# Four row tiles: adding the bonus term on TensorE, copying out on ScalarE, loading g as one row, and a new order of the steps

## The chip, the cores and the metric

The kernel runs on one core of a Trainium2 chip. The core has five engines that run side by side and meet only through semaphores: TensorE (PE in the profile; it multiplies matrices and writes the results to PSUM), VectorE (DVE), ScalarE (ACT), GpSimd (POOL) and SyncE (SP, which here only issues DMAs). The metric is the device time of one execution in microseconds. The median of three runs of the kernel before is 148.79 us (148.41 to 152.24).

## The reference

Two layers, one after the other. The first is a linear attention with a decaying state, over 4 batches, 8 heads, 768 positions and a head size of 48:

```
for t in range(S):
    cur = einsum('bhd,bhe->bhde', u * k[t], v[t])
    y[t] = einsum('bhd,bhde->bhe', r[t], state + cur)
    state = w * state + einsum('bhd,bhe->bhde', k[t], v[t])
x = y, heads side by side: (4, 768, 384)
```

The second normalises each row of x and puts it through two matrices:

```
xn = (x - mean(x)) / sqrt(var(x) + 1e-6) * g_ln
out = x + relu(xn @ w_ch1) @ w_ch2        # 384 -> 1536 -> 384
```

All inputs and the output are fp32.

## The kernel before

**Tiling.** The 4 x 768 rows are cut into 24 chunks of 128 rows, 6 to a batch. Within a chunk the recurrence is solved by matrix products: k and r are scaled by powers of w (steps SK, SR), turned so that the head size lies on the partitions (TRk, TRr on TensorE with a copy out by TCk, TCr, or TDk, TDr by DMA), multiplied (AT) and masked (AM); S builds what the chunk adds to the state, ZU and ZD scale it, and Y multiplies masked products and state with v. What position t itself gives through u is a number cc per row and head (made by TensorE from q = k * r in S, copied out by CC2), times v: that product is Vb (step VB2). Step X adds Vb to y while copying y out of PSUM, with the sum of each row as by-product in sm; the result is x. Chunks are loaded in pairs. The first two pairs (chunks 0 to 3) have a layout of their own, in which a partition holds two neighbouring rows; their steps have a 2 at the end of the name (AT2, AM2, Y2, SR2, SK2; for the first pair SRH and SKH, by halves).

**The second layer.** SQ (ACT) takes the sum of squares of x minus the mean, RS the root, XN makes the centred x in bf16, LT and XT turn it (or LTD by DMA); chunks are grouped by one or two (GROUPS). UP multiplies with w_ch1, RL applies the relu out of PSUM into hT, DN multiplies hT with w_ch2, OT scales by RS and adds x, STO stores. UP,16*g+m is the m-th tile of 512 columns of group g; DN,4*i+d is the d-th third of the sum of chunk i. w_ch1 is loaded in three thirds by LW1 on SP's queue and scaled by -g in nine pieces by SW (piece 3*n+kc belongs to third n), on the engine that the plan names. w_ch2 is loaded in three thirds by IW2 on POOL's queue, with a conversion to bf16. g is loaded by LG (line 218) as 128x3, one element at a time, and negated by UGC (line 304).

**The order.** PLAN (lines 18 to 67) is a list of 755 steps, each with a name, an index and an engine (v DVE, s ACT, g POOL, - for TensorE or SP's queue). The kernel is emitted in just this order, so each engine's and each queue's own order is the order of its steps in the list; nothing is reordered later. DU,n is filler for TensorE: n/512 products of 128x512 zeros on line 279. Work ahead of the first UP is called the prologue below.

**Buffers.** The names y, o, hp and at are PSUM tiles: one buffer each for y and o, two each for hp and at. S and Y share y; UP, the products Y2 and the early rows WBM (line 288, an fp32 product that spreads ln w over 128 partitions) and COL (line 315, small fp32 products that turn rows into columns) share hp; AT, AT2 and all transpositions share at. A step that writes such a buffer waits for the readers of the tile before in it. The SBUF rings have the lengths in SLOTS.

**Lines.** Line 205 holds all products of two tensors (SK, SR, Q2, ZU), 200 and 202 all copies on ACT and on DVE or POOL, 342, 344 and 346 SW on ACT, DVE and POOL, 492 VB2, 590 X, 597 SQ, 646 UP, 674 DN. w_f and w_sb in the rows are the fp32 and bf16 weights.

Of the kernel before, what the change touches and what calls it, by code (L numbers as in the profile page):

```python
# [32 lines left out]
DN,2,- RS,2,g LT,5,- S,7,- OT,0,v RL,66,s UP,49,- XN,6,s XT,5,v UP,50,- RL,49,v TCr,4,s LR2,6,- DN,4,- ZU,7,v UP,80,-
ZD,7,v LK,10,- CV2,4,g RL,50,v Y,7,- RL,80,s DN,5,- X,7,v LV,13,- DN,6,- Q2,4,v XN,7,s UP,65,- SQ,4,s OT,1,v LV,11,-
AT,8,- SQ,6,s SR2,6,v AT,9,- DN,8,- RS,6,s LR2,5,- AM,8,v RS,4,s DN,9,- SQ,7,s LK,11,- S,8,- DN,10,- ZU,8,v LV,10,-
UP,82,- CC2,4,s OT,2,v VB2,4,g LK,12,- LT,6,- AM,9,v Y,8,- RL,82,s DN,12,- STO,0,- RL,65,s SK,10,g DN,13,- XT,6,v LK,13,-
X,8,v DN,14,- ZD,8,g LV,12,- S,9,- UP,96,- OT,3,v SK,11,g ZU,9,v UP,98,- RL,96,s SR2,5,v Y,9,- TDk,5,- SQ,8,s DN,16,-
CV2,5,v LT,7,- TRr,5,- SK,12,v DN,17,- X,9,v TCr,5,s RL,98,v LK,15,- UP,97,- XN,9,g LK,14,- XT,7,v ZD,9,g UP,81,- RL,97,s
LR2,7,- XN,8,s SK,13,g UP,112,- RL,81,s LTD,8,- DN,18,- RS,7,s Q2,5,v TRr,6,- OT,4,v UP,114,- SK,15,g TCr,6,s RL,112,v STO,1,-
S,10,- CV2,6,g DN,20,- CC2,5,s TDk,6,- RL,114,s SK,14,v AT,10,- RS,5,s AT,11,- ZU,10,v DN,21,- SR2,7,g AM,10,v UP,113,- STO,3,-  # L40
DN,22,- AM,11,v RL,113,s TDk,7,- Y,10,- VB2,5,g UP,129,- OT,5,v TRr,7,- RL,129,s LR,19,- UP,130,- ZD,10,g X,10,v UP,133,- LV,14,-
Q2,6,v RL,130,s DN,24,- TCr,7,v STO,2,- S,12,- DN,25,- CC2,6,s LV,15,- XN,10,s VB2,6,g ZU,12,v AT,12,- SQ,9,s AT,13,- STO,5,-
AM,12,v Y,11,- RL,133,s DN,26,- Q2,7,g LK,16,- X,11,v UP,128,- OT,6,v XN,11,s Y,12,- UP,131,- X,12,v LK,17,- DN,28,- AM,13,v
SR,19,g CV2,7,s S,13,- DN,29,- LTD,9,- ZU,13,v SQ,12,s DN,30,- ZD,13,g RL,128,s Y,13,- OT,7,v AT,15,- SQ,11,s LR2,8,- AT,14,-
X,13,v UP,132,- STO,4,- SK,17,g RL,131,v SQ,13,s LR,18,- S,14,- AM,15,v LV,17,- XN,13,s DN,32,- LV,16,- XN,12,s DN,33,- ZU,14,v
RL,132,s SK,16,v UP,144,- CC2,7,v AM,14,v LTD,10,- VB2,7,g UP,147,- RL,144,s DN,34,- SQ,10,s SR2,8,v TDk,8,- Y,14,- RS,8,s UP,145,-
RL,147,s OT,8,v TRr,8,- ZD,14,v UP,148,- TCr,8,s RL,145,v RL,148,v DN,36,- LK,18,- X,14,v DN,37,- CV2,8,v XN,14,s S,15,- UP,149,-
ZU,15,v LK,19,- UP,161,- ZD,15,g RL,149,v LV,18,- DN,38,- RL,161,s Q2,8,v STO,7,- Y,15,- LV,20,- UP,146,- SK,18,g X,15,v STO,6,-
AT,16,- RL,146,s AT,17,- XN,15,v LR,20,- UP,164,- RS,9,g OT,9,v LTD,11,- AM,17,v UP,160,- RL,164,s RS,10,g DN,40,- RL,160,v S,16,-
SK,19,v UP,163,- SR,18,v CC2,8,s TDk,9,- UP,165,- ZU,16,v RL,163,s AM,16,v DN,41,- ZD,16,g RL,165,s DN,42,- VB2,8,g LR,21,- UP,162,-  # L50
OT,10,v TDr,9,- Y,16,- RL,162,v DN,44,- X,16,v DN,45,- XN,16,g UP,176,- LV,19,- SR,20,g DN,46,- RL,176,s STO,8,- Y,17,- OT,11,v
UP,178,- LK,20,- X,17,v DN,48,- Q2,9,v LK,21,- UP,177,- XN,17,g SR,21,v DN,49,- LTD,12,- RL,177,s RL,178,v DN,50,- CV2,9,v AT,19,-
OT,12,v AT,18,- SK,20,g STO,9,- UP,180,- AM,18,v STO,11,- S,18,- SK,21,g RL,180,s UP,181,- CC2,9,v ZU,18,v DN,52,- VB2,9,g AM,19,v
# [4 lines left out]
UP,210,- AM,21,v RL,208,s DN,64,- SR,22,v S,20,- RL,210,v UP,212,- TDr,11,- CC2,10,v DN,65,- SK,22,v VB2,10,g ZU,20,v DN,66,- Y,20,-
TDk,11,- OT,16,v UP,209,- X,20,v DN,68,- RL,209,s ZD,20,v STO,14,- S,21,- XN,20,g RL,212,v CV2,11,s DN,69,- LTD,14,- ZU,21,v SQ,20,s
DN,70,- UP,213,- RS,13,s OT,17,v STO,16,- UP,211,- STO,15,- Y,21,- RL,211,s DN,72,- X,21,v DN,73,- Q2,11,v SQ,21,s AT,23,- ZD,21,v  # L60
RL,213,s AT,22,- XN,21,v S,22,- LTD,15,- UP,224,- ZU,22,v AM,22,v DN,74,- ZD,22,g RL,224,s UP,226,- CC2,11,s RS,14,s OT,18,v VB2,11,g
# [721 lines left out]
```

## Time and profile before

| | before |
|---|---|
| median of three runs | 148.79 us |
| profiled execution | 149.24 us |
| its span, first to last instruction | 147.5 us |
| TensorE busy | 141.5 us (96%) |
| VectorE busy | 112.3 us (76%) |
| ScalarE busy | 82.4 us (56%) |
| GpSimd busy | 72.0 us (49%) |
| share of the DMA engines, SP's queue | 78.3% |
| instructions | 4689 |

All rows are from one profiled execution; its span is 1.74 us shorter than its time. The ends of matmuls are modelled, so busy time of TensorE is not time at its peak: the distance from the start of one to the start of the next says more. A row of the order in time has start, length, engine, line, operation, result and operands, and how many were merged; in brackets stands the engine's idle time before it and what ended it.

### The profile page before, as it was taken

What the parts mean: (1) busy time and instruction counts of PE and PEld (TensorE: products, weight loads), DVE (VectorE), ACT (ScalarE), POOL (GpSimd) and SP (SyncE); (2) the same over time, 40 slices, a digit from 0 to 9 for tenths busy, and PEclk for the clock granted to TensorE, in tenths of its full rate; (3) what the DMA queues carried; (4) which work ended last, traced back from release to release, by engine and by line L of the source; (5) the groups of instructions that cost most, each with busy time, mean ns of one, the idle gap of its engine ahead of it and who ended that gap; (6) DMA issues with size and microseconds to landing.
All of it is one profiled execution on the core that took longest, in us unless ns stands there. A gap on an engine that the chain in (4) does not pass through costs nothing.

```text
span 147.5 us, 4689 instructions
## 1 busy us (share of the span) xinstructions
PE 141.5 (96%) x1943; PEld 111.1 (75%) x1943; DVE 112.3 (76%) x206; ACT 82.4 (56%) x181; POOL 72.0 (49%) x96
## 2 busy tenths in 40 slices
...
GB/s 112 300 242 240 192 339 187 283 243 215 220 95 231 202 225 165 264 205 258 164 192 196 195 235 124 173 204 227 197 112 191 182 142 154 82 46 119 8 99 111
DMA packets 85097, 27.18 MB, mean 184 GB/s; under 512 B 80338, under 2 KB 83540, under 8 KB 85076
## 3 DMA queue, kind: packets, MB, share of 16 engines
q1 hardware_dynamic: 84642, 25.70, 78.3%
...
q8 instruction: 15, 0.25, 0.7%
q14 instruction: 6, 0.05, 0.1%
q10 hardware_dynamic: 2, 0.00, 0.0%
HBM read 18.88 MB, written 4.72 MB: 160 GB/s over the span
## 4 chain that ended last, share of the span: by engine, by line
PE 65%; SPq 13%; DMA 11%; DVE 6%; POOL 1%; issue 1%; DVEq 0%
PE o L674 28%; PE hp L646 25%; DMA kf<-in_k_dram 6%; DMA w_f<-in_moe_w_ch_dram 5%; SPq L374 4%; SPq L352 3%; PE at L544 3%; PE y L583 2%; SPq L358 2%; PE y L481 2%; PE y L575 2%; SPq L371 1%; SPq L377 1%; DVE hT L664 1%; PE y L460 1%
## 5 line engine op out<-in xcount | busy, mean ns | idle before, releaser
L646 PE MATMUL hp<-xT,w_sb 128*128 128x128 bf16 (+1 forms) x648 | 57.1, 237 | 0.8 <-ACT w_sb L342 0.7
L662 ACT ACTIVATE hT<-hp 128x512 bf16<-128x512 f32 x55 | 32.4, 594 | 40.5 <-PE hp L646 39.7
L646 PEld LDWEIGHTS <-w_sb 128*128 128x128 bf16 x648 | 49.3, 114 | 5.1 <-ACT w_sb L342 1.3
L674 PE MATMUL o<-w_sb,hT 128*128 128x384 bf16 x276 | 53.0, 326 | 0.0
L674 PEld LDWEIGHTS <-hT 128*128 128x128 bf16 x276 | 25.0, 97 | 12.0
L553 DVE TENSOR_TENSOR A<-at,mask 128x1024 bf16<-128x1024 f32 x20 | 24.2, 1216 | 2.1 <-PE at L544 2.1
L492 POOL TENSOR_TENSOR Vb<-vf,cc 128x768 f32<-128x768 f32 x11 | 16.5, 1498 | 14.9 <-ACT cc L200 8.5
L730 DVE SCALAR_TENSOR_TENSOR ot<-o,rs,x 128x384 f32<-128x384 f32 x23 | 14.1, 615 | 12.3 <-PE o L674 7.0
L205 POOL TENSOR_TENSOR sk<-kf,Fk 128x384 bf16<-128x384 f32 x13 | 13.6, 1053 | 8.5 <-DMA kf<-in_k_dram 7.9
L597 ACT ACTIVATE sqj<-x,sm 128x384 bf16<-128x384 f32 x24 | 14.6, 609 | 2.2 <-DVE x L590 2.2
L205 POOL TENSOR_TENSOR Z<-ZS,WLZ 128x384 bf16<-128x384 f32 x8 | 8.0, 1002 | 15.4 <-DVE ZS L565 15.4
L590 DVE SCALAR_TENSOR_TENSOR x<-y,Vb 128x384 f32<-128x384 f32 x20 | 11.0, 552 | 4.5 <-PE y L583 4.1
L664 DVE TENSOR_SCALAR hT<-hp 128x512 bf16<-128x512 f32 x17 | 11.5, 684 | 3.4 <-PE hp L646 3.3
L279 PE MATMUL o<-warm 128*128 128x512 bf16 x33 | 11.3, 427 | 1.0 <-DVE warm L228 1.0
L200 ACT COPY trr<-at 128x512 bf16<-128x512 bf16 (+1 forms) x13 | 9.1, 764 | 4.4 <-PE at L400 4.4
L205 DVE TENSOR_TENSOR sr<-rf,Fr 128x768 bf16<-128x768 f32 (+1 forms) x11 | 9.5, 870 | 1.6 <-DMA rf<-in_r_dram 1.6
L205 POOL TENSOR_TENSOR sr<-rf,Fr 128x384 bf16<-128x384 f32 (+1 forms) x5 | 6.6, 1325 | 7.0 <-DMA rf<-in_r_dram 7.0
L604 ACT ACTIVATE xn<-x,sm 128x384 bf16<-128x384 f32 x13 | 7.8, 609 | 2.3 <-DVE x L590 2.3
L606 POOL TENSOR_SCALAR xn<-x,sm 128x384 bf16<-128x384 f32 x8 | 5.3, 665 | 7.6 <-DVE x L590 7.5
L205 DVE TENSOR_TENSOR q<-trk,trr 128x1024 bf16<-128x1024 bf16 x9 | 7.5, 837 | 1.4 <-ACT xn L604 1.0
L481 PE MATMUL y<-vv,sk 128*128 128x96 bf16 (+1 forms) x96 | 7.3, 204 | 0.3 <-ACT vv L200 0.2
L205 DVE TENSOR_TENSOR sk<-kf,Fk 128x384 bf16<-128x384 f32 (+1 forms) x10 | 7.4, 747 | 0.0
...
## 6 DMA issues: line engine op xcount, KB each, us to landing
...
rf<-in_r_dram SPq DMA_DIRECT2D x9, 384.0 KB, 4.7
...
w_sb<-in_moe_w_ch_dram POOLq DMA_DIRECT2D x3, 384.0 KB, 6.0
...
kf<-in_k_dram SPq DMA_DIRECT2D x2, 384.0 KB, 4.5
```

The lines of the kernel that those rows point to most:

```text
L205: engines[e].tensor_tensor(out=out, in0=in0, in1=in1, op=ALU.mult)
L279: nc.tensor.matmul(out=warm_ps[0][:].rearrange("p (a t) -> p a t", a=4), lhsT=warm[:], rhs=rhs, start=True, stop=True)
L481: nc.tensor.matmul(out=t[:, q * E2 : (q + 1) * E2].rearrange("p (e d) -> p e d", e=2), lhsT=lhs, rhs=rhs, start=first, stop=True, skip_gro ...
L492: engines[e].tensor_tensor(out=Vb2(g).rearrange("p (x h d) -> p x h d", x=2, h=H), in0=vals, in1=cc2(g)[:].unsqueeze(3).to_broadcast([P, 2 ...
L553: nc.vector.tensor_tensor(out=AA(i)[:].rearrange("p e q t -> p (e q) t"), in0=psum["at", i][:].rearrange("p e q t -> p (e q) t"), in1=mask ...
L590: nc.vector.scalar_tensor_tensor(out=xx(i)[:], in0=psum["y", i][:, :C], scalar=1.0, in1=Vb(i), op0=ALU.mult, op1=ALU.add, accum_out=sm[i][:],)
L597: nc.scalar.activation(out=sqj[:], in_=xx(i)[:], func=ACT.Square, bias=sm[i][:], scale=-float(C), accum_out=sq[g][:, j : j + 1])
L646: nc.tensor.matmul(out=t[:, a * gw : (a + 1) * gw], lhsT=w1_sb[n][kc][:, fb::FB], rhs=xT(g)[:, :size, kc, :], start=(kc == 0), stop=(kc == ...
L662: nc.scalar.activation(out=o, in_=s, func=ACT.Relu)
L664: nc.vector.tensor_relu(out=o, in_=s)
L674: nc.tensor.matmul(out=psum["o", i][:, :C], lhsT=hT(g)[:, fk, j * P : (j + 1) * P], rhs=w2_sb[d][:, a, :], start=(fk == 0), stop=(fk == FK ...
L730: nc.vector.scalar_tensor_tensor(out=ot(i)[:], in0=psum["o", i][:, :C], scalar=rs[g][:, j : j + 1], in1=xx(i)[:], op0=ALU.mult, op1=ALU.add,)
```

## The change

1. Chunks 0 to 3 (VPE = 4): a new step YV multiplies Vb with an fp32 identity on TensorE and adds it into the PSUM tile of y. X of these chunks is now an ACT copy out of PSUM, with the row sum as by-product; on other chunks X is as before. The identity is made on POOL by MF.
2. g is loaded as one row of 384 into a tile that is used only later (the last buffer of ot); three fp32 products of one column each in COL turn it into 128x3 in PSUM, from where UGC negates it.
3. The plan is another one: 757 steps, in a new order, with many steps on other engines, and other amounts of filler.

```diff
+VPE = 4
 PLAN = """
-WF,0,s MP,1,g LK2,0,- MW,0,v ML,0,v MM2,0,g DU,3072,- UF,0,- TL,0,s MO,0,v MZ,0,v LR2,0,- LR2,1,- MP,2,g MP,0,g LK2,1,-
-LN,0,s MI2,0,g MP,5,g MP,3,g WBM,0,- MP,4,g LG,0,- MM,0,g LV2,0,- DU,4096,- UWR,0,v FR2,0,s MI,0,g FR2,1,s LR2,2,- SRH,0,v
-FK2,0,s SRH,1,v FK2,1,s SKH,0,v LK,5,- FK,0,s TRr,0,- SKH,1,v DU,1024,- TCr,0,s SR2,1,v TRk,0,- LR2,3,- DU,512,- SK2,1,v COL,0,-
-TCk,0,s TRr,1,- LV2,1,- CV2,0,s UW,0,v Q2,0,v AT2,0,- DU,1536,- FR,0,s TCr,1,v LK,4,- WL,0,s SR2,2,g AM2,0,v S,0,- AT2,1,-
-LK,6,- CC2,0,s DU,512,- ZU,0,v TRk,1,- AM2,1,v DU,512,- VB2,0,g S,1,- TCk,1,s LK,7,- DU,512,- TRr,2,- LW1,1,- SR2,3,v DU,512,-
-Y2,1,- TCr,2,s LW1,2,- LV,5,- Q2,1,v Y2,0,- SK,4,g ZU,1,v UGC,0,s LV,4,- CV2,1,s X,1,v TRr,3,- SK,5,g X,0,v DU,512,-
-AT2,3,- TCr,3,s DU,512,- AM2,3,v SK,7,g S,2,- XN,1,s AT2,2,- XN,0,g CC2,1,v ZU,2,v SQ,1,s DU,512,- VB2,1,g TRk,2,- AM2,2,v
-S,3,- LW1,0,- TCk,2,s DU,512,- SK,6,v LT,1,- Y2,2,- SQ,0,s SW,5,g XT,1,v SW,3,s LV,6,- LT,0,- SW,4,v TRk,3,- Q2,2,g
-ZU,3,v DU,1024,- SW,6,s LK,8,- XT,0,v Y2,3,- SW,7,s TCk,3,v X,2,v SW,8,s AT,5,- AT,4,- X,3,v XN,2,g DU,512,- UP,2,-
-AM,5,v XN,3,s IW2,0,g LV,7,- UP,1,- RL,2,s Q2,3,g AM,4,v LT,2,- CV2,2,s DU,512,- UP,17,- RL,1,s XT,2,v S,4,- RL,17,s
-LR2,4,- UP,34,- SW,0,v SW,2,s AT,6,- CC2,2,v ZU,4,v SW,1,s VB2,2,g AT,7,- AM,6,v LK,9,- Y,4,- RL,34,s UP,0,- IW2,1,g
-X,4,v UP,18,- RL,0,s AM,7,v IW2,2,g Y,5,- XN,4,s LT,3,- UP,32,- RL,18,s RS,1,g LV,8,- X,5,v LT,4,- UP,33,- RL,32,s
...
+WF,0,s MF,0,g LK2,0,- MW,0,v MP,5,v ML,0,v DU,3072,- LG,0,- TL,0,s MM,0,g MP,1,v MO,0,v UF,0,- MP,2,g LR2,0,- MM2,0,g
+LK2,1,- LN,0,s LR2,1,- MI2,0,g WBM,0,- MP,0,g LV2,0,- MI,0,g DU,4608,- FR2,0,s UWR,0,v FK2,0,s LV2,1,- SRH,0,v FR2,1,s MZ,0,v
+FK2,1,s SRH,1,v COL,0,- LR2,2,- SKH,0,v DU,512,- SKH,1,v TRr,0,- MP,3,v DU,2048,- LR2,3,- SR2,1,v TCr,0,s TRk,0,- SK2,1,v FR,0,s
+DU,512,- LV,5,- TRr,1,- WL,0,s CV2,0,g TCk,0,v DU,3072,- TCr,1,s LK,5,- Q2,0,v CV2,1,g UW,0,v AT2,0,- FK,0,s AT2,1,- AM2,0,v
+LK,4,- DU,1536,- UGC,0,s SR2,2,g S,0,- LK,6,- AM2,1,v DU,512,- TRk,1,- LK,7,- DU,1536,- ZU,0,v CC2,0,v TCk,1,v TRr,2,- VB2,0,g
+LW1,2,- S,1,- TCr,2,s LW1,0,- Y2,0,- LV,4,- SR2,3,v Y2,1,- LW1,1,- SK,4,g ZU,1,v LV,6,- AT2,3,- TRr,3,- Q2,1,v YV,0,-
+MP,4,g AM2,3,v TCr,3,s SK,7,g DU,512,- S,2,- SK,6,v X,0,s AT2,2,- ZU,2,v DU,512,- XN,0,g AM2,2,v CC2,1,s TRk,3,- VB2,1,g
+YV,1,- TCk,3,s S,3,- LK,8,- X,1,s SK,5,v Y2,2,- Q2,3,v SQ,1,s XN,1,g LT,0,- SW,2,v TRk,2,- IW2,0,g XT,0,s YV,2,-
+TCk,2,v SW,7,g LV,7,- LT,1,- Y2,3,- X,2,s XT,1,v Q2,2,v SW,8,s XN,2,g AT,4,- ZU,3,v AT,5,- SW,1,s CV2,2,g AM,4,v
+YV,3,- SW,6,s LK,9,- DU,512,- SW,0,v S,4,- X,3,s SW,3,v UP,18,- ZU,4,v DU,512,- AM,5,v CC2,2,s SW,5,s UP,0,- VB2,2,g
+RL,18,s LT,2,- Y,4,- LR2,4,- RL,0,s XT,2,v UP,2,- SW,4,v IW2,1,g X,4,v DU,512,- AT,6,- RL,2,s LR2,5,- AT,7,- XN,4,g
+UP,32,- AM,7,v IW2,2,g CV2,3,s Y,5,- DN,0,- XN,3,g RL,32,v SK,9,g X,5,v UP,17,- XN,5,v SK,8,g UP,1,- AM,6,v RL,17,s
...
+    ident_f = const.tile([P, P], FP32, name="ident_f")
...
-    g_p = const.tile([P, CK], FP32, name="g_p")
+    g_row = ot(SLOTS["ot"] - 1)[0:1, :]
...
-        queues[e].dma_start(out=g_p[:], in_=moe_g_ln.rearrange("(kc p) -> p kc", p=P))
+        queues[e].dma_start(out=g_row, in_=moe_g_ln.rearrange("(o c) -> o c", o=1))
...
+    def MF(i, e):
+        nc.gpsimd.memset(ident_f[:], 0.0)
+        nc.gpsimd.affine_select(
+            out=ident_f[:], in_=ident_f[:], compare_op=ALU.not_equal, fill=1.0, base=0,
+            pattern=[[-1, P]], channel_multiplier=1,
+        )
...
-        nc.scalar.mul(out=g_neg[:], in_=g_p[:], mul=-1.0)
+        nc.scalar.mul(out=g_neg[:], in_=psum["g"], mul=-1.0)
...
+        for kc in range(CK):
+            nc.tensor.matmul(
+                out=psum["g"][:, kc : kc + 1], lhsT=g_row[:, kc * P : (kc + 1) * P], rhs=ones[0:1, 0:1],
+                start=True, stop=True,
+            )
...
+    def YV(i, e):
+        nc.tensor.matmul(
+            out=psum["y", i][:, :C], lhsT=ident_f[:], rhs=Vb(i), start=False, stop=True, skip_group_check=True
+        )
+
     def X(i, e):
+        if i < VPE:
+            nc.scalar.activation(out=xx(i)[:], in_=psum["y", i][:, :C], func=ACT.Identity, accum_out=sm[i][:])
+            return
```

More of the change, by code (lines that the diff above doesn't have):

```diff
@@ L33 @@
[L33 to L53, printed above, removed]
@@ L58 @@
[L58 to L61, printed above, removed]
@@ new lines @@
+X,6,v SR2,5,g TRr,4,- RL,33,s DN,4,- LV,9,- SQ,6,s S,7,- DN,5,- SQ,3,s ZU,7,v LR2,6,- UP,66,- TCr,4,v Y,7,- LK,10,-
+DN,6,- RL,66,v LK,11,- Q2,4,g UP,50,- X,7,v LV,11,- CV2,4,s AT,9,- RL,50,v AT,8,- UP,64,- OT,1,v ZD,7,g UP,65,- AM,9,v
+RL,64,s LK,13,- S,8,- SQ,7,s SR2,6,g ZU,8,v DN,8,- RS,6,s LR2,7,- AM,8,v RL,65,s UP,82,- CC2,4,s XN,6,s TRr,5,- RL,82,v
+RS,4,s RS,3,g UP,49,- LV,10,- TCr,5,s ZD,8,v LT,6,- DN,9,- SK,11,g STO,0,- UP,81,- RL,49,s VB2,4,g SQ,5,s DN,10,- LK,15,-
+RL,81,s Y,8,- OT,2,v UP,80,- XT,6,s LK,12,- SK,13,g X,8,v DN,12,- SQ,8,s SK,10,v S,9,- DN,13,- RS,5,g ZU,9,v RL,80,s
```

48 lines of the change are left out of this document (35 added, 13 removed).

## The prediction

> **What bounds it now.** I read the busy time by stretches first, then TensorE's instructions in order of time. Stretches (us, length, PE busy, weight loads, DVE, ACT, POOL, clock, DMA share, GB/s):
>
> ```profile
> 0.00:26.10 26.10, 24.09 (x418) 15.40 (x419) 20.62 (x44) 16.88 (x30) 15.62 (x34) 1.00 0.90 229
> 26.10:28.58 2.48, 1.75 (x24) 1.48 (x25) 2.30 (x4) 2.15 (x4) 2.45 (x4) 1.00 0.90 309
> 28.58:44.00 15.42, 15.37 (x268) 13.74 (x267) 11.29 (x23) 12.71 (x28) 8.96 (x13) 1.00 1.00 200
> 44.00:144.40 100.40, 100.31 (x1240) 80.48 (x1237) 77.69 (x138) 50.69 (x121) 45.00 (x47) 1.00 0.81 171
> ```
>
> From 28.58 us to the last product TensorE has nothing left to gain: idle 0.05 and 0.09 us. Ends of matmuls are modelled, so I also took the distance from start to start against the pace of the same operation elsewhere; that finds 0.9 us lost in these 116 us. So the end is the moment when this dense stretch begins, plus a fixed amount of work. DVE, ACT and POOL have room there. What can move the time lies ahead of it. In order of time (start, length, engine, line; in brackets the idle time and its releaser):
>
> ```profile
> 0.97 2.74 PE L279 MATMUL o<-warm 128*128 128x512 bf16 x6 [0.97 <-DVE warm L228]
> 3.51 1.20 PE L288 MATMUL hp<-ln_all,ones 128*128 128x384 f32 x2
> 4.55 1.89 PE L279 MATMUL o<-warm 128*128 128x512 bf16 x8
> 6.88 0.77 PE L400 MATMUL at<-ident,sr 128*128 128x128 bf16 x8 [0.45 <-DVE sr L205]
> ...
> 8.74 0.52 PE L315 MATMUL hp<-ones,ln_all 1*48 1x1 f32 x16
> 9.12 0.50 PE L315 MATMUL hp<-ones,uw_row 1*48 1x1 f32 x16
> ...
> 10.11 0.44 PE L443 MATMUL at<-trr,trk 48*64 48x128 bf16 x16
> ...
> 13.54 0.32 PE L468 MATMUL y<-Z,ident 128*128 128x384 bf16 x1
> ...
> 22.64 0.34 PE L631 MATMUL at<-ident,xn 128*128 128x128 bf16 x3
> ...
> 25.12 0.62 PE L544 MATMUL at<-trr,trk 48*128 48x128 bf16 x16
> 25.67 0.39 PE L279 MATMUL o<-warm 128*128 128x512 bf16 x1
> 26.10 0.25 PE L646 MATMUL hp<-xT,w_sb 128*128 128x128 bf16 x1
> 26.71 0.25 PE L646 MATMUL hp<-xT,w_sb 128*128 128x128 bf16 x1 [0.37 <-ACT w_sb L342]
> 27.33 1.42 PE L646 MATMUL hp<-xT,w_sb 128*128 128x128 bf16 x22 [0.36 <-ACT w_sb L342]
> 28.58 0.33 PE L631 MATMUL at<-ident,xn 128*128 128x128 bf16 x3
> ```
>
> The first UP starts at 26.10 and its first two products wait for scaled weights: 24 products in 2.48 us, where 24 take 1.34 in the row of the chain below, so 1.1 us are lost. Up to 26.10 the starts show 2.7 us of waiting, beside the 0.97 at the front. All idle time of TensorE that any change could win back is 2.7 + 1.1 + 0.9 = 4.7 us.
>
> ```profile
> 138.46 1.34 PE hp L646 x24
> 139.80 1.95 PE o L674 x12
> ```
>
> **What TensorE gets to do besides.** The filler group has this row:
>
> ```profile
> L279 PE MATMUL o<-warm 128*128 128x512 bf16 x33 | 11.3, 427 | 1.0 <-DVE warm L228 1.0
> ```
>
> The new order holds DU for 39 products instead of 33 (19968 columns against 16896, 512 each), all six more ahead of the first UP. Early ones take 0.42 us (six from 0.97 to 3.51); later ones 0.22 (25.67 is held up; the eight at 4.55 take 0.23). So +1.3 us. They are in TensorE's own order and cost this whether or not they are needed as filler.
>
> Each of the four YV is an fp32 product of 128x384 against a 128x128 identity: just the shape of L288, which took 1.04 us to the next start. That is the upper end. The lower: L288 is two products in the trace, and one bf16 product of 384 columns takes 0.163 (12 in 1.95), so 0.33. L288 ran where the filler sped up from 0.42 to 0.22; scaled by that it is 0.53. I take 0.7, between the scaled row and the row: 4 x 0.7 = 2.8 us (1.3 to 4.2). The Trainium skill, "FP8 and Floating Point Precision", section TensorE Precision Notes, says that true fp32 takes four passes through the array; with the 0.163 that would be 0.65 each and 2.6 in all, an estimate that no row here separates from mine.
>
> The three products that turn g cost 0.1 (16 of the same kind in COL took 0.38, from 8.74 to 9.12). The rest of the work is the same set of steps. Sum: **+4.2 us** on TensorE against at most 4.7 us of idle time to put it in. With every wait gone the gain would be 0.5 us; with none gone the loss 4.2.
>
> **Which waits go.** The 1.1 us at the first UP go. w is now loaded in the order 2, 0, 1, and the first UP needs third 2:
>
> ```profile
> 23.37 0.49 DVE L344 TENSOR_SCALAR w_sb<-w_f,g_neg 128x512 bf16<-128x512 f32 x1 [0.18 <-DMA w_f<-in_moe_w_ch_dram]
> 25.32 1.95 ACT L342 ACTIVATE w_sb<-w_f,g_neg 128x512 bf16<-128x512 f32 x3 [1.31 <-DMA w_f<-in_moe_w_ch_dram]
> 29.41 0.87 DVE L344 TENSOR_SCALAR w_sb<-w_f,g_neg 128x512 bf16<-128x512 f32 x1
> ```
>
> The thirds land at about 23.3, 25.3 and 29.4. The queue has moved the same bytes ahead of the first (one chunk of v more, 192 KB), so I keep these times. But then the first UP is ready on the weights' side near 25.5 and TensorE isn't there yet.
>
> g as one row saves SP time, 1.40 against 0.46 for the row u of the same kind, and takes the place ahead of r:
>
> ```profile
> 1.25 0.46 SPq L215 DMA_DIRECT2D u_row<-in_u_dram  x1
> ...
> 4.66 1.40 SPq L218 DMA_DIRECT2D g_p<-in_moe_g_ln_dram  x1
> ```
>
> That puts the first r 0.5 us later (it is waited for at 6.88, through sr) and what stands behind g 0.9 earlier. v of the second pair moves up four transfers. I count the two ends, -0.9 and +0.5, as nothing, since SP isn't what the first UP now waits for.
>
> **Which waits come.** DVE, ACT and POOL rows of before:
>
> ```profile
> 1.74 0.38 DVE L269 MEMSET WLZ<- 128x384 f32 x1
> 8.63 1.01 ACT L200 COPY trk<-at 128x1024 bf16<-128x1024 bf16 x1
> 8.93 0.95 DVE L205 TENSOR_TENSOR sk<-kf,Fk 128x768 bf16<-128x768 f32 x1
> 11.48 1.21 DVE L525 TENSOR_TENSOR A<-at,mask 128x1024 bf16<-128x1024 f32 x1
> 17.20 0.54 DVE L590 SCALAR_TENSOR_TENSOR x<-hp,Vb 128x384 f32<-128x384 f32 x1
> 19.58 0.61 ACT L597 ACTIVATE sqj<-x,sm 128x384 bf16<-128x384 f32 x1
> 20.09 0.20 ACT L597 ACTIVATION_READ_ACCUMULATOR sqj<-x,sm 128x1 f32 x1
> 21.03 1.48 POOL L492 TENSOR_TENSOR Vb<-vf,cc 128x768 f32<-128x768 f32 x1
> 21.33 1.59 DVE L205 TENSOR_TENSOR sk<-kf,Fk 128x384 bf16<-128x384 f32 x1
> ...
> 32.09 1.12 POOL L349 DMA_DIRECT2D w_sb<-in_moe_w_ch_dram  x2
> 40.48 0.81 PE L674 MATMUL o<-w_sb,hT 128*128 128x384 bf16 x4
> ```
>
> 1. TCk0 leaves ACT (8.63) for DVE, behind SR2 and SK2 of pair 1, which end at 9.88 in before and about 1 us later in after (r late by 0.5, the memset of WLZ, 0.38, put between the two SRH). It ends near 11.7, so AT2 starts at 11.8 to 12.3 instead of 10.11. The fillers stand there now, but S0, A and ZU0 on DVE, and S1 behind ZU0, follow at about the same distance: S1 at 15.6 instead of 13.54, 2 us late.
> 2. X0 to X3 have YV and the new copy in their way. On DVE x took 0.54; on ACT I price it by the SQ row at 0.61 and 0.20 for the sum (bounds 0.5 to 0.9). X0 stands behind VB2, Y2, AT2 and a transposition: 19.6 instead of 17.20. LT0 then comes near 24 instead of 22.64. This takes 4 x 0.54 from DVE, but TCk of three pairs, Q2 of two, SK5, SW2 and SW3 come to DVE there, and only TCr1, TCk3 and XT0 leave it besides: ahead of the first UP DVE isn't relieved.
> 3. AT4 needs TCk2, which stands on DVE behind SW2, and that waits for the second third of w (25.3): TCk2 ends near 26.5 to 27, so TensorE waits 0.2 to 0.7.
> 4. Adding up TensorE's order by these starts, the first UP comes at 29 instead of 26.10. Less the 1.1 us it no longer loses and 0.5 for S4, now ahead of it, the dense stretch is 1.3 us late, if nothing runs slower than alone.
> 5. It won't all run as alone. SK at 21.33 took 1.59 for 384 columns where 768 took 0.95 at 8.93: it stood until Vb on POOL ended at 22.51. The conversion of v of pairs 0 to 2 moves to POOL (0.82 us each by POOL's row at 43.00, below), next to SR2, SK2, Q2 on DVE. One or two such stops on the chain of points 1 to 3: 0.7 us (0 to 2). The Trainium skill, "SBUF — State Buffer", section Who interferes with whom, says that a DVE instruction with two SBUF inputs contends with a GpSimd one that reads SBUF, and that one blocks fully; the SK row agrees.
> 6. SW3 on DVE waits for the last third of w (29.4), and behind it stand AM5, XT2, SW4, X4, which AT6, UP32 and Y5 wait for: 0.8 us (0 to 1.6). w2's first load now goes out before SW7 and shares the DMA engines with that third.
> 7. POOL issues the last load of w2 behind XN4, near 35.5, where before both went at 32.09. It lands some 6 us after (the profile's table of DMA issues gives 6.0). DN2, at 40.48 in before, would come near 41: 0.4 us (0 to 1.5).
>
> ```profile
> 43.00 0.82 POOL L202 CAST vv<-vf 128x768 bf16<-128x768 f32 x1
> w_sb<-in_moe_w_ch_dram POOLq DMA_DIRECT2D x3, 384.0 KB, 6.0
> ```
>
> Later, an order that has to be as dense as the old one over 100 us; I add 0.3 (0 to 1.5). **Sum:** 1.3 + 0.7 + 0.8 + 0.4 + 0.3 = +3.5 us. By the other count: 4.2 added, 1.1 and 2.3 of the 2.7 us won back, 2.7 of new waits (0.5 at point 3, 1.9 at 5 to 7, 0.3). The profiled execution took 149.24 with a span of 147.5; it would be 151.0 and 152.7. The three runs' median, 148.79, is 0.45 below the profiled one, so I forecast **152.3**.
>
> **Rivals.** *The cover holds.* The six fillers and YV fall into time that TensorE would have waited anyway, and points 5 to 7 come to nothing: +1.3 or less, down to the floor of -0.5, so 148.3 to 150.1; with half of 5 to 7 about 151. For it: the weights come at 25.3, and TensorE waited 3.8 us up to 28.58. Against: point 4 adds the list with hardly any gap left in it. It decides for not slower when the first UP starts before 27.5. A change within 2% (about what a measurement of this kernel can tell from no change, 3.0 us here) has 0.40.
> *POOL and DVE block each other, or w's last third is late.* Points 5 to 7 at their upper ends, 2 + 1.6 + 1.5 in place of 1.9: +6.7, 155.5. For it: the 1.59 row, and POOL has six more steps, among them SK8 beside SK9. Against: DVE had many pairs of that kind in before too. 0.13.
> *It relieves nothing.* That x leaves DVE is worth nothing, since DVE isn't what the dense stretch waits for (77.69 us of 100.40): this is in the forecast already, has no chance of its own, and is why I see no gain to weigh against the 4.2.
> Faster by over 2% would take a span under 144.5, 2 us below the floor of no waits at all; only if YV cost a third of what I think and the idle time vanished would it come near: 0.03.
>
> **Numbers.** My forecast, slower by 2 to 4%, has 0.44; with the rival above it slower by over 2% has 0.57. Same 0.40, faster 0.03. The range takes the floor below and the blocked case above, 148.6 to 156.0; 1 in 10 is left out on each side at most.
>
> **What would show it.** Right: six more products on L279; YV with 0.5 to 0.8 us each; the first UP at 28 to 30.5; no wait for w_sb there; TensorE dense behind 37 or so. Wrong: the first UP before 27.5, YV over 1 us, DVE's fp32 products of 1.5 us in a row, or waits of TensorE behind 45 us, which before doesn't have.

## The result and the profile after

The changed kernel takes **152.66 us** (median of four runs, 151.37 to 153.83); beside it, on the same chip, the kernel before took 148.71 (148.41 to 152.24). The ratio is **1.026, 95% interval 1.021 to 1.031**: slower, and 0.4 us above the forecast of 152.3. Ratios, here and below, leave out disturbed runs of either kernel, so they are not always the quotient of the medians; the profiles of the two runs with g as one row on the old order are of such runs, with the clock at 0.99 over the span.

| | before | after |
|---|---|---|
| profiled execution, us | 149.24 | 151.37 |
| its span, us | 147.5 | 149.6 |
| first UP starts, us | 26.10 | 29.39 |
| TensorE busy, us | 141.5 | 144.8 |
| VectorE busy, us | 112.3 | 113.3 |
| ScalarE busy, us | 82.4 | 79.3 |
| GpSimd busy, us | 72.0 | 81.9 |

The profiled execution is the fastest of the four; the other three have spans of 150.3, 151.4 and 152.1.

The page of after, its busy times, its chain by engine and the filler group:

```profile
PE 144.8 (97%) x1963; PEld 114.0 (76%) x1963; DVE 113.3 (76%) x201; ACT 79.3 (53%) x179; POOL 81.9 (55%) x105
PE 88%; DMA 5%; DVE 4%; issue 1%; POOL 0%; DVEq 0%
L288 PE MATMUL o<-warm 128*128 128x512 bf16 x39 | 12.3, 427 | 1.0 <-DVE warm L230 1.0
```

TensorE is busy 3.3 us longer and idle 1.2 us less (span less busy time is 6.0 before, 4.8 after): together the 2.1 us by which the span grew. So by this account the loss is work on TensorE, and not waiting of TensorE. Whether the time comes back when the work is taken out again is another question, which the experiments ask.

Busy time of after by stretches (columns as in the prediction):

```profile
0.00:29.10 29.10, 28.12 (x447) 18.34 (x448) 23.02 (x43) 16.00 (x32) 18.42 (x37) 1.00 0.97 255
29.10:32.00 2.90, 2.83 (x55) 2.58 (x52) 2.90 (x7) 1.94 (x6) 1.28 (x1) 1.00 0.98 197
32.00:44.00 12.00, 11.27 (x181) 9.46 (x180) 9.98 (x18) 7.96 (x20) 8.30 (x12) 1.00 1.17 198
44.00:60.00 16.00, 16.00 (x240) 13.33 (x238) 13.41 (x26) 9.86 (x25) 12.29 (x13) 1.00 0.85 184
```

The prologue is now full: 28.12 of 29.10 us, and 0.97 of the rest is the wait at the very front. From 32 to 44 TensorE has waits that add up to 0.73; behind 44 there is none.

TensorE's instructions of after in order of time:

```profile
0.97 2.74 PE L288 MATMUL o<-warm 128*128 128x512 bf16 x6 [0.97 <-DVE warm L230]
3.51 1.49 PE L297 MATMUL hp<-ln_all,ones 128*128 128x384 f32 x2
4.79 2.40 PE L288 MATMUL o<-warm 128*128 128x512 bf16 x9
7.12 0.82 PE L323 MATMUL hp<-ones,ot 1*128 1x1 f32 x6
7.87 0.52 PE L331 MATMUL hp<-ones,ln_all 1*48 1x1 f32 x16
...
12.72 0.67 PE L459 MATMUL at<-trr,trk 48*64 48x128 bf16 x32
...
16.46 0.33 PE L484 MATMUL y<-Z,ident 128*128 128x384 bf16 x1
...
19.69 0.86 PE L606 MATMUL hp<-Vb,ident_f 128*128 128x384 f32 x2
20.39 0.38 PE L288 MATMUL o<-warm 128*128 128x512 bf16 x1
...
24.85 0.34 PE L655 MATMUL at<-ident,xn 128*128 128x128 bf16 x3
...
27.35 0.62 PE L560 MATMUL at<-trr,trk 48*128 48x128 bf16 x16
27.90 0.91 PE L606 MATMUL hp<-Vb,ident_f 128*128 128x384 f32 x2
28.65 0.38 PE L288 MATMUL o<-warm 128*128 128x512 bf16 x1
28.86 0.34 PE L476 MATMUL y<-uwI,q 128*128 128x2 bf16 x8
29.39 0.83 PE L670 MATMUL hp<-xT,w_sb 128*128 128x128 bf16 x12
...
38.16 0.33 PE L655 MATMUL at<-ident,xn 128*128 128x128 bf16 x3 [0.48 <-DVE A L569]
...
41.10 0.81 PE L698 MATMUL o<-w_sb,hT 128*128 128x384 bf16 x4 [0.24 <-DMA w_sb<-in_moe_w_ch_dram]
```

Behind the 0.97 no row up to the first UP at 29.39 carries a wait. YV goes from 19.69 to 20.39, 0.70 for one. The six records of the g products go from 7.12 to 7.87, 0.75 in all. The first UP doesn't wait for weights. Two waits stand further on, and the chain of work that ended last runs through the second; this is its part in front of DN2 (start, length, what):

```profile
32.39 0.56 DVE x L614 x2
32.96 0.10 issue
33.06 0.54 POOL xn L630
33.60 7.46 DMA w_sb<-in_moe_w_ch_dram
41.06 0.04 issue
41.10 0.81 PE o L698 x4
```

X4 on DVE, XN4 on POOL, then POOL issues the last third of w2, which lands 7.46 us later, 0.04 before DN2.

The other engines of after:

```profile
10.87 0.69 DVE L204 COPY trk<-at 128x1024 bf16<-128x1024 bf16 x1 [0.53 <-PE at L416]
16.29 1.47 POOL L508 TENSOR_TENSOR Vb<-vf,cc 128x768 f32<-128x768 f32 x1 [2.26 <-DVE cc L204]
16.73 1.85 DVE L207 TENSOR_TENSOR sr<-rf,Fr 128x768 bf16<-128x768 f32 x1
21.12 0.52 ACT L612 ACTIVATE x<-hp 128x384 f32<-128x384 f32 x1
21.49 0.23 ACT L612 ACTIVATION_READ_ACCUMULATOR x<-hp 128x1 f32 x1
24.87 0.81 DVE L360 TENSOR_SCALAR w_sb<-w_f,g_neg 128x512 bf16<-128x512 f32 x1
29.02 0.87 DVE L360 TENSOR_SCALAR w_sb<-w_f,g_neg 128x512 bf16<-128x512 f32 x2
```

The scaling of w on DVE (24.87, 29.02) waits for no load. TCk0 on DVE (10.87) waits for TensorE, and not TensorE for it. SR2 at 16.73 took 1.85 where SK2, of the same size and kind, took 0.95 at 8.93 in before: VB2 runs on POOL from 16.29 to 17.76. How full DVE is between 12 and 33 us, before:

```profile
12.00:33.00 21.00, 19.92 (x428) 15.13 (x424) 18.92 (x34) 15.45 (x30) 17.07 (x15) 1.00 0.98 248
```

and after:

```profile
12.00:33.00 21.00, 20.93 (x429) 15.46 (x429) 20.03 (x31) 12.31 (x28) 14.45 (x14) 1.00 1.01 253
```

DVE has 1.1 us more to do there than before, while ACT has 3.1 and POOL 2.6 less.

### The profile page after: what moved, and what is told of

It reads as the page before. It is cut to its first block, busy times and chain, and to the rows that moved or that the text cites. A ratio compares the mean times of both kernels' runs of the same rounds, so it can differ in the third digit from the quotient of the medians.

```text
span 149.6 us, 4727 instructions
## 1 busy us (share of the span) xinstructions
PE 144.8 (97%) x1963; PEld 114.0 (76%) x1963; DVE 113.3 (76%) x201; ACT 79.3 (53%) x179; POOL 81.9 (55%) x105
## 4 chain that ended last, share of the span: by engine, by line
PE 88%; DMA 5%; DVE 4%; issue 1%; POOL 0%; DVEq 0%
PE o L698 30%; PE hp L670 28%; PE o L288 7%; DMA w_sb<-in_moe_w_ch_dram 5%; PE at L416 4%; PE at L560 3%; PE y L497 3%; PE y L599 2%; PE hp L520 2%; PE y L591 2%; DVE A L569 2%; PE hp L606 1%; PE y L476 1%; PE hp L297 1%; PE at L459 1%; PE hp L713 1%
## 5 line engine op out<-in xcount | busy, mean ns | idle before, releaser
L686 ACT ACTIVATE hT<-hp 128x512 bf16<-128x512 f32 x51 | 30.0, 593 | 37.4 <-PE hp L670 37.1
L698 PEld LDWEIGHTS <-hT 128*128 128x128 bf16 x276 | 24.8, 97 | 12.3 <-issue 0.4
L508 POOL TENSOR_TENSOR Vb<-vf,cc 128x768 f32<-128x768 f32 x8 | 11.8, 1476 | 17.5 <-ACT cc L202 9.7
L688 DVE TENSOR_SCALAR hT<-hp 128x512 bf16<-128x512 f32 x21 | 14.4, 688 | 5.3 <-PE hp L670 5.1
L207 POOL TENSOR_TENSOR Z<-ZS,WLZ 128x384 bf16<-128x384 f32 x10 | 10.2, 1022 | 10.0 <-DVE ZS L581 10.0
L288 PE MATMUL o<-warm 128*128 128x512 bf16 x39 | 12.3, 427 | 1.0 <-DVE warm L230 1.0
L207 POOL TENSOR_TENSOR sr<-rf,Fr 128x768 bf16<-128x768 f32 (+1 forms) x7 | 11.9, 1699 | 2.4 <-DMA rf<-in_r_dram 2.4
L207 DVE TENSOR_TENSOR sr<-rf,Fr 128x384 bf16<-128x384 f32 (+1 forms) x9 | 7.3, 823 | 1.5 <-DMA rf<-in_r_dram 1.5
L581 DVE TENSOR_TENSOR ZS<-y,Z 128x384 f32<-128x384 f32 x12 | 6.6, 553 | 2.2 <-PE y L497 2.0
L640 POOL TENSOR_SCALAR rs<-sq 128x1 f32<-128x1 f32 (+1 forms) x10 | 2.8, 278 | 10.1 <-ACT sqj L621 9.5
L204 POOL CAST vv<-vf 128x768 bf16<-128x768 f32 x6 | 5.3, 899 | 5.1 <-DMA vf<-in_v_dram 4.7
L207 POOL TENSOR_TENSOR q<-trk,trr 128x1024 bf16<-128x1024 bf16 x3 | 6.4, 2133 | 3.0 <-DVE trr L204 2.6
```

The lines of the kernel that those rows point to most:

```text
L207: engines[e].tensor_tensor(out=out, in0=in0, in1=in1, op=ALU.mult)
L288: nc.tensor.matmul(out=warm_ps[0][:].rearrange("p (a t) -> p a t", a=4), lhsT=warm[:], rhs=rhs, start=True, stop=True)
L508: engines[e].tensor_tensor(out=Vb2(g).rearrange("p (x h d) -> p x h d", x=2, h=H), in0=vals, in1=cc2(g)[:].unsqueeze(3).to_broadcast([P, 2 ...
L686: nc.scalar.activation(out=o, in_=s, func=ACT.Relu)
L688: nc.vector.tensor_relu(out=o, in_=s)
L698: nc.tensor.matmul(out=psum["o", i][:, :C], lhsT=hT(g)[:, fk, j * P : (j + 1) * P], rhs=w2_sb[d][:, a, :], start=(fk == 0), stop=(fk == FK ...
```

## The experiments

Two explanations were open at first. One is **the list** (theory 1): TensorE has no gap ahead of the first UP, so what was added to its list is the loss, and what is taken out comes back. The other is **the chain on DVE** (theory 2): TCk, Q2 and the scaling of w came to DVE, its chain of small steps is what is late, and the filler only fills the holes that it leaves. Later a third came up (theory 3), that both end at the same moment and each covers what the other loses.

The slow early products end at another moment in each profile: the g products behind them start at 7.12 in after, and between 6.52 and 7.74 in the runs that keep the same 15 early fillers. A difference of that size between the first UPs of two profiles needn't come from the edit. So the distance from the start of the g products to the first UP is given too; in after it is 22.27.

**Filler out.** Only the first two fillers, 15 products, stay.

```diff
-DU,512,- ... DU,2048,- ... DU,512,- ... DU,3072,- ... DU,1536,- ... DU,512,- ... DU,1536,-
-DU,512,- ... DU,512,- ... DU,512,- ... DU,512,- ... DU,512,-
```

> The changed kernel without its last 24 filler products (all DU behind the first two steps of them; 22 stand ahead of the first UP). Theory 1, TensorE's own list sets when the first UP starts: the list is 4.8 us shorter there, so the first UP moves from 29.4 to the next limit, between 25 and 27.5, and the time falls by 2 to 4.5 us, to 148 to 150.5. Theory 2, waits on DVE, POOL and the weights set it and the filler only lies in them: the same time within 0.7 us, 152 to 153.3, with idle time where the filler was.

Measured: 152.93 us (152.32 to 153.46), 1.027 (1.017 to 1.037): no gain. One stretch of this run:

```profile
10.00:20.00 10.00, 7.56 (x155) 6.06 (x156) 8.90 (x13) 3.84 (x8) 8.10 (x7) 0.73 1.03 240
```

Of 24 products, 5.3 us at 0.22, TensorE gained nothing: from 10 to 20 us it is busy for 7.56 of 10, and the granted clock falls to 0.73. The first UP starts at 30.51, behind 29.39. Filler as a whole isn't ballast, and this run can't tell the list from the chain, because it changes the clock as well.

**YV out, x back on DVE**, in the new order with its filler.

```diff
-VPE = 4
+VPE = 0
-MF,0,g ... YV,0,- ... YV,1,- ... YV,2,- ... YV,3,-
```

> The changed kernel without the first part: no YV, x of chunks 0 to 3 on DVE with Vb added there, all else and the order as changed. Theory 1: the four YV, 0.70 us each, come off: 2.5 to 3 us faster than the changed kernel, 149.6 to 150.2. Theory 2: nothing or slower, as DVE gets 4 x 0.55 more ahead of the first UP: 152 to 154.

Measured: 152.24 us (151.48 to 153.71), 1.024 (1.010 to 1.038), the first UP at 29.01. The 2.85 us of YV are gone and the first UP is only 0.38 earlier; from the g products (6.52) it is 22.49, so of the 2.85 nothing arrives. Three waits stand in their place:

```profile
22.19 0.32 PE L483 MATMUL y<-Z,ident 128*128 128x384 bf16 x1 [0.41 <-ACT cc L201]
...
25.14 0.34 PE L654 MATMUL at<-ident,xn 128*128 128x128 bf16 x3 [0.56 <-POOL xn L629]
...
28.20 0.35 PE L475 MATMUL y<-uwI,q 128*128 128x2 bf16 x8 [0.72 <-DVE Z L206]
```

and DVE is busy from 12 to 33 us for 20.93 of 21:

```profile
12.00:33.00 21.00, 19.13 (x405) 14.98 (x405) 20.93 (x37) 9.13 (x19) 14.68 (x14) 0.92 1.05 264
```

So in the new order, putting x back on DVE costs about what YV costs, and a shorter list alone doesn't bring the first UP forward. The clock granted in this stretch is 0.92, so a part of what didn't come back may be the clock's.

**The order alone:** no YV, x on DVE, g as 128x3, and no filler behind the first 15 products.

```diff
-VPE = 4
+VPE = 0
-MF,0,g ... DU,... (twelve) ... YV,0,- ... YV,3,-
-        queues[e].dma_start(out=g_row, in_=moe_g_ln.rearrange("(o c) -> o c", o=1))
+        queues[e].dma_start(out=g_p[:], in_=moe_g_ln.rearrange("(kc p) -> p kc", p=P))
... (the three products in COL out, UGC from g_p)
```

> The new order alone: no YV, x on DVE, g loaded as 128x3 as before, and no filler behind the first two steps of it. Theory 1: 4.8 of filler, 2.8 of YV and 0.75 of the products for g come off the list; the waits then bind, and the time is 146 to 148.5, at or below the kernel before. Theory 2: the new order's waits hold it at 151 or more.

Measured: 154.45 us (152.71 to 154.59), 1.035 (1.022 to 1.048), the slowest of all. The granted clock by slices of 3.8 us:

```profile
PEclk9996555699999999999999999999999999999999
```

About half the clock from 15 to 27 us. What the list would be worth without YV and filler can't be had this way.

**YV in bf16.** Vb of chunks 0 to 3 is stored as bf16, and the identity of the transpositions is used.

```diff
-            out=psum["y", i][:, :C], lhsT=ident_f[:], rhs=Vb(i), start=False, stop=True, skip_group_check=True
+            out=psum["y", i][:, :C], lhsT=ident[:], rhs=Vh(i), start=False, stop=True, skip_group_check=True
```

> The changed kernel with Vb of chunks 0 to 3 written as bf16 and YV as a bf16 product with the bf16 identity (Vb is rounded to bf16). ACT's copy stays. YV costs 0.16 instead of 0.70. Theory 1: 2.1 us faster, 150.2 to 150.8. Theory 2: within 0.7 us of the changed kernel.

Measured: 151.86 us (150.70 to 152.72), 1.022 (1.007 to 1.038), the first UP at 28.75. YV falls from 0.70 to about 0.17 each, 2.1 us in all. The first UP is 0.64 earlier, and 0.53 counted from the g products (7.01). A wait has taken the place of 0.91 of the rest; it stands within the products of Y2:

```profile
24.70 0.36 PE L521 MATMUL hp<-vv,A 64*64 64x48 bf16 x11 [0.91 <-issue]
```

The profile names nothing that these products wait for: A, which they read, was made on DVE from 21.87 to 23.08. What held them stays open.

**TCk back on ACT.** If the chain on DVE is the bound, this relieves it.

```diff
-TCk,0,v ... TCk,1,v ... TCk,2,v
+TCk,0,s ... TCk,1,s ... TCk,2,s
```

> The changed kernel with TCk of pairs 0 to 2 back on ACT; TensorE's list is untouched. It takes 2.0 us from DVE ahead of the first UP. Theory 1, TensorE's list alone sets the first UP (it had no gap up to 29.39): no more than 0.6 us against the changed kernel, the first UP at 29 to 29.5. Theory 2, DVE's chain sets it and the list merely has the same length: the first UP at 28 to 28.5 and 1 us or more gained.

Measured: 152.47 us (151.46 to 153.35), 1.017 (1.010 to 1.023), the first UP at 30.82, 23.85 from the g products (6.97), so 1.58 later than in after. TensorE now waits for a copy on ACT, and then for uwI, which stands behind q on DVE:

```profile
12.51 2.13 DVE L207 TENSOR_TENSOR q<-trk,trr 128x1024 bf16<-128x1024 bf16 x1 [2.10 <-ACT trk L202]
...
13.44 0.44 PE L459 MATMUL at<-trr,trk 48*64 48x128 bf16 x16 [0.44 <-ACT trr L202]
...
14.94 0.34 PE L476 MATMUL y<-uwI,q 128*128 128x2 bf16 x8 [0.30 <-DVE uwI L204]
```

A copy of that size took 1.01 on ACT (the ACT row of before at 8.63) and 0.69 on DVE. And q, which took 0.69 in after, took 2.13 here, beside SR2 on POOL from 12.28 to 14.09, and ended at 14.64, 0.55 behind it: the blocking of point 5 of the prediction, this time on the way to the first UP. So back on ACT the copies are no gain, and the move to DVE wasn't the mistake that point 1 took it for. That the chain on DVE is no bound isn't shown by this run, because q became slower along with the edit.

**Both: YV in bf16 and TCk on ACT.**

```diff
-TCk,0,v ... TCk,1,v ... TCk,2,v
+TCk,0,s ... TCk,1,s ... TCk,2,s
-            ... lhsT=ident_f[:], rhs=Vb(i), ...
+            ... lhsT=ident[:], rhs=Vh(i), ...
```

> Both relieved: YV as bf16 products (Vb of chunks 0 to 3 rounded to bf16), 2.15 us off TensorE's list, and TCk of pairs 0 to 2 back on ACT. Theory 3, the list and DVE's chain end together and each hides what the other loses: the first UP at 27 to 27.7 and 2 us less than the changed kernel, where YV in bf16 alone gave 0.8. If something else holds it (the weights, ACT): as with bf16 alone, the first UP at 28.5 or later.

Measured: 152.08 us (150.85 to 152.94), 1.013 (1.006 to 1.019), the first UP at 30.58, 0.24 earlier than with TCk on ACT alone. But the g products start at 7.74 here and at 6.97 there: counted from them it is 22.84, 1.01 earlier, so about half of YV's 2.1 us arrives. Of the rest 0.70 stands directly ahead of the first UP, in S4 behind the conversion of v that came to POOL:

```profile
30.41 0.33 PE L498 MATMUL y<-vv,sk 128*128 128x96 bf16 x4 [0.70 <-POOL vv L205]
```

The first UP at 27 to 27.7 that theory 3 asked for didn't come: copies on ACT are no relief.

**Part 1 alone on the old order:** each YV is put directly ahead of its X, and X goes to ACT.

```diff
+VPE = 4
-X,1,v ... X,0,v ... X,2,v ... X,3,v
+YV,1,- X,1,s ... YV,0,- X,0,s ... YV,2,- X,2,s ... YV,3,- X,3,s
```

> The kernel before with the first part alone: YV ahead of X for chunks 0 to 3, x on ACT, the fp32 identity on POOL; order, filler and g as before. 2.8 us more on TensorE's list, against 2.7 + 1.1 us of idle time there. Theory 1: 1 to 2.2 us slower than before, the first UP near 27.5. Rival: the idle time takes it, within 0.5 us of before; or DVE's relief of 4 x 0.55 makes it faster by up to 1 us.

Measured: 150.86 us (150.27 to 152.05), **1.015 (1.011 to 1.019)**: slower by itself.

```profile
16.75 0.91 PE L599 MATMUL hp<-Vb,ident_f 128*128 128x384 f32 x2
17.50 0.61 PE L409 MATMUL at<-ident,sr 128*128 128x128 bf16 x8
...
28.37 1.50 PE L663 MATMUL hp<-xT,w_sb 128*128 128x128 bf16 x24
```

YV is 0.75 to the next start here, and the four are 0.70 to 0.85, 3.05 in all. The first UP moves from 26.10 to 28.37, by 2.27 of them; the first transposition starts at 6.88 and 6.86, so the early products have no part in it. The 24 products of L663 end in 1.34 (29.71 is the next start), so the 1.1 us of waiting for weights are gone: the first UP comes later than the weights. This is the trade of the prediction without the new order.

**Part 2 alone on the old order:** g as one row.

```diff
-        queues[e].dma_start(out=g_p[:], in_=moe_g_ln.rearrange("(kc p) -> p kc", p=P))
+        queues[e].dma_start(out=g_row, in_=moe_g_ln.rearrange("(o c) -> o c", o=1))
```

> The kernel before with the second part alone: g loaded as one row, three products more in COL (0.75 us in the changed kernel), UGC from PSUM. SP is free 0.9 us earlier behind it. Theory: between -0.5 and +0.6 us of before; the list is 0.75 us longer, and the weights come up to 0.9 us earlier.

Measured: 148.95 us (148.19 to 151.45), **0.994 (0.990 to 0.998)**. The g products cost TensorE the same here as in after, 0.75 (the next start is 9.79):

```profile
9.04 0.82 PE L314 MATMUL hp<-ones,ot 1*128 1x1 f32 x6
```

That it gains in spite of these 0.75 us must come from the queue that g no longer holds up (1.40 us before); this is argued and wasn't shown, and the next run doesn't repeat the gain.

**The same with the negation of g earlier**, right behind WL, since TensorE waited 0.33 for it in the run above.

```diff
-UGC,0,s            (behind ZU,1)
+UGC,0,s            (behind WL,0)
```

> The kernel before with g as one row, and its negation (UGC) right behind WL instead of behind TCr2, so that the PSUM buffer that g is in comes free before Y2 wants it (0.33 us of waiting there with g as one row alone). It should be as fast as that kernel or up to 0.4 us faster: 0.3 to 1% below before. If the gain of that kernel was chance: within 0.3% of before.

Measured: 149.57 us (147.87 to 154.31), 0.997 (0.991 to 1.002): no difference from before. Part 2 is worth something between nothing and 1%; no run here beats the kernel before by more.

**After once more, unchanged**, for the spread of its runs.

> The changed kernel once more, beside the next three on the same chip. 2.0 to 3.2% slower than before. TensorE's filler turns from 0.42 to 0.22 us per product at another moment in each execution (the nine products after L297 took 2.33 us to the next start in its profile, 2.04 to 2.95 in the others); as nothing waits ahead of the first UP, the first UP moves with it: 22.3 us after the end of these nine, within 0.3.

Measured: 152.63 us (150.60 to 153.20), 1.019 (1.010 to 1.026). The first UP starts at 29.56; the filler in front of the g products ended 0.16 later than in the first execution (7.28 and 7.12), and everything up to the first UP moved by that: 22.28 and 22.27 us between the two. The span is 151.1, 1.5 longer. The chain names the rest:

```profile
33.76 8.76 DMA w_sb<-in_moe_w_ch_dram
42.53 0.04 issue
42.57 0.81 PE o L698 x4
```

The last third of w2 was issued 0.16 later and took 8.76 us to land in place of 7.46. 0.16 and 1.30 are the 1.5 us.

**Ten products of filler out**, all ahead of the first AT2.

```diff
-DU,4608,- ... DU,2048,- ... DU,512,- ... DU,3072,-
+DU,4096,- ... DU,1024,-
```

> The changed kernel without ten of the filler products ahead of AT2 (11 left there, as in the kernel before); all later filler stays, so the clock should hold. Theory 4: the delay is made in the first 13 us, where filler holds AT2 back and DVE's chain of A, Z, q starts behind it (DVE idle 0.71 us for it), so list and chain both move: AT2 about 1.2 us earlier, the first UP at 28 to 28.4, 1.0 to 1.4 us faster than the changed kernel. Rival: the later waits on DVE take it all, as without YV: within 0.4 us of the changed kernel.

Measured: 150.87 us (150.16 to 151.19), **1.010 (1.005 to 1.015)**, 1.8 below the median of after on the same chip: the best of the new order, though its interval still overlaps that of after (1.010 to 1.026). The granted clock stays at 1.00. But the first UP starts at 29.02, only 0.4 to 0.5 earlier, for 2.2 us of filler. The first half of AT2 starts at 11.04, the second waits for ACT until 12.44. In after both halves run from 12.72 without a gap, which puts the second near 13.0 (an estimate, half of the 32 products): so that half came only some 0.6 earlier.

```profile
11.04 0.44 PE L459 MATMUL at<-trr,trk 48*64 48x128 bf16 x16
12.44 0.44 PE L459 MATMUL at<-trr,trk 48*64 48x128 bf16 x16 [0.96 <-ACT trr L202]
...
40.16 0.81 PE L698 MATMUL o<-w_sb,hT 128*128 128x384 bf16 x4
```

The rest of the gain is in the last row: DN2 waits for nothing here. It starts 0.94 ahead of where it does in the first execution of after and 2.41 ahead of the second. The last third of w2 went out at 33.23, 0.4 to 0.5 ahead of after, and landed within 6.4 us, against 7.46 and 8.76; whether the shorter landing comes from the edit isn't known.

**Ten products out and YV in bf16.**

```diff
-DU,4608,- ... DU,2048,- ... DU,512,- ... DU,3072,-
+DU,4096,- ... DU,1024,-
-            ... lhsT=ident_f[:], rhs=Vb(i), ...
+            ... lhsT=ident[:], rhs=Vh(i), ...
```

> As a_fill10, and YV as bf16 products (Vb of chunks 0 to 3 rounded). Theory 4: the chain is earlier by 1.2 us and the list by 3.3 us: the first UP at 27 to 27.6, 1.6 to 2.4 us faster than the changed kernel. Rival: no better than YV in bf16 alone, 0.8 us.

Measured: 151.07 us (150.73 to 151.81), 1.013 (1.007 to 1.018), the first UP at 28.47. Over 4 us of TensorE's list are gone, and the first UP is 0.92 earlier than in after. From the g products (6.60) it is 21.87. With the list shortened that far, something else ends near 28.5: TensorE waits 0.42 for trk from DVE and 0.59 for trr from ACT at AT2, 0.87 within Y2 again without a named cause, and 0.21 for Z from DVE. How much of the bound is DVE's, how much ACT's or POOL's, and what stands behind the unnamed wait, no run separates.

**DN2 as a meeting point.** In all ten profiles of the new order, span less the start of DN2 is 108.4 to 108.6 us. So whatever these kernels differ by is decided by then, and three things decide it: when the first UP starts, what TensorE waits for behind it, and when the last third of w2 lands.

| | g products | first UP | DN2 starts | DN2 waits for w2 | span |
|---|---|---|---|---|---|
| after | 7.12 | 29.39 | 41.10 | 0.24 | 149.6 |
| after, again | 7.28 | 29.56 | 42.57 | 1.35 | 151.1 |
| ten products out | 6.88 | 29.02 | 40.16 | none | 148.8 |
| ten out, YV in bf16 | 6.60 | 28.47 | 40.45 | none | 149.0 |
| YV in bf16 | 7.01 | 28.75 | 40.41 | none | 148.9 |
| YV out | 6.52 | 29.01 | 41.18 | none | 149.7 |
| TCk on ACT | 6.97 | 30.82 | 42.99 | 0.87 | 151.5 |
| TCk on ACT, YV in bf16 | 7.74 | 30.58 | 42.67 | 0.82 | 151.2 |

Issuing that load ahead of XN4 wasn't tried.

## Why the prediction was right, and where its steps were not

The side and the time hold, and the trace of after bears the mechanism out: TensorE had little to gain, got more work, and the first UP was late by 3.3 us where 2.9 were forecast. The list ahead of the first UP differs from before by six fillers, four YV, the g products and S4, and the slow early pace lasted longer: 1.3 + 2.85 + 0.75 + 0.53 + 0.5 = 5.9. The first UP moved by 3.29, so some 2.6 us of waiting were filled, nearly all of the 2.7 that the prediction found there. Part 1 alone on the old order shows the same trade by experiment. That the added work is the only cause of the delay in the new order isn't shown, and the runs speak against it: taken out again, YV in bf16 brought 0.5 of 2.1 us at the first UP and ten fillers 0.4 of 2.2. What came up in their place were waits for steps on DVE, ACT and POOL, and 0.9 of a wait without a named cause. Term by term:

- **Six more fillers, +1.3.** Six more there are, 39. The nine early ones have 2.40 where eight had 1.89, and WBM goes from 3.51 to 4.79 where it ended at 4.55: the early slow pace lasted longer, by 0.5 in all. But the forecast that they cost this "whether or not they are needed" is too simple: without ten of them the first UP came only 0.4 earlier, and without 24 the clock fell.
- **YV, 0.7 each.** 0.70, 0.70, 0.70 and 0.75: 2.85. The Trainium skill, "FP8 and Floating Point Precision", section TensorE Precision Notes, says four passes for true fp32, from which the prediction estimated 0.65; the trace is 0.05 to 0.10 above it and agrees.
- **The g products, 0.1: the term that was mis-sized most.** They took 0.75. It was priced by products with 48 columns of weights, 16 in 0.38; the 16 are records, two to a product, and these have 128 columns: 125 ns for each of six records in place of 24. That the columns make the difference wasn't tested. TensorE's additions are 4.9 in place of 4.2, without the 0.5 of the slow pace.
- **The wait for weights, 1.1, goes.** It went. The order 2, 0, 1 was not needed for that: in the run with part 1 alone it went too.
- **Point 1, TCk0 on DVE holds AT2.** The time was near (12.72 against 11.8 to 12.3; S1 16.46 against 15.6), but the reason was wrong. TCk0 waited 0.53 for TensorE, and with ten fillers fewer the first half of AT2 starts at 11.04 and the second waits for ACT. In after the list held AT2; ACT's copy for its second half ended at 12.63, some 0.4 ahead of that half. And back on ACT the copies were worse.
- **Point 2, X0 at 19.6.** It started at 21.12, for it stands behind all that was late already. Its price, 0.61 and 0.20, was 0.52 and 0.23. That DVE isn't relieved is so: from 12 to 33 us it was busy for 18.92 us in before and 20.03 in after.
- **Point 3, AT4 waits for TCk2, 0.2 to 0.7.** No wait: AT4 at 27.35 has none. SW2 ran at 24.87 without waiting, so the second third was there ahead of the 25.3 that I had kept.
- **Point 4, the first UP at 29.** 29.39.
- **Point 5, blocking, 0.7.** The blocked products are there (SR2 1.85 at 16.73). But TensorE waited for none of them up to 29.39: the full list covered them. With TCk on ACT it did wait behind a blocked q.
- **Point 6, the last third of w, 0.8.** Nothing: SW3 at 29.02 didn't wait for it. The landing times of before were kept for loads that now stand elsewhere in the queue: the last third went out from 17.86 in place of 19.57, and at 7.8 us to landing (9.8 in before) it was in near 25.7 and not at 29.4.
- **Point 7, the last third of w2, 0.4 (0 to 1.5).** 0.24 in one execution and 1.35 in another. The mechanism and its bounds were right. Its two parts were off to both sides (the load went out at 33.60 where 35.5 was forecast, and took 7.46 where 6.0 was). It is worth more than its 0.4: the chain runs through it, and most of the difference between two executions of after is its landing time.
- **Later, 0.3.** 0.48 at 38.16, behind A on DVE.

The balance: the first UP 3.29 later, 1.1 of that won back at the weights and 0.53 by S4, which now stands ahead (28.86 to 29.39), and 0.24 and 0.48 of new waits make +2.4; the span grew by 2.1, and 0.3 stay unassigned. That the forecast came within 0.4 is partly luck. Like for like it was 1.3 too high: it gave the profiled execution 152.7 and a span of 151.0, and that one took 151.37 with 149.6; points 5 and 6, 1.5 too much, outweigh the 0.7 missing for what TensorE got. But the median of after lies 1.3 above its profiled execution, where that of before lay below; in the other profile of after, a difference of that size is the landing time of w2.

*The cover holds* fell by its own mark: it needed the first UP before 27.5. *POOL and DVE block each other* fell for the changed kernel: the blocked rows exist and cost TensorE nothing there. *It relieves nothing* holds: DVE has 1.1 us more to do from 12 to 33 us than before.

What the parts are worth, as far as the runs go: part 1 alone +1.5%, part 2 alone 0 to -1%, the new order with part 2 and its filler but without YV +2.4%, everything together +1.9 to +2.6%. They don't add up. The likely reason, by the waits that come up when the list is shortened, is that in the new order TensorE's list and the steps on the other engines end at nearly the same moment.
